# Summing the value rows' squares in the token stage, and the gate's logits right behind the taps

## The chip, the cores and the metric

The kernel runs on one core of one Trainium2 chip. The time is that of one execution on the device in microseconds; three runs of the kernel before gave 1456.38 to 1456.81 us, with a median of 1456.58 us. The engines are called by the profile's names: PE is TensorE, DVE VectorE, ACT ScalarE, POOL GpSimd, and SP is the queue that issues nearly all DMA transfers. PEld is PE's loading of weights.

## The reference

Two branches read the same tokens x (2048 x 576, float32) and are mixed by a gate. Cut to what matters:

```python
g = sigmoid((x * gate_w).sum(-1, keepdims=True))        # one logit per token
# branch a: a state space convolution, by FFT
P = exp(dt * A * l);  K = einsum("dn,dnl,dn->dl", C, P, dt * B).real
a = irfft(rfft(x, 2L) * rfft(K, 2L))[:L] + x * Dskip
# branch b: product key experts, 32 heads, 64 x 64 = 4096 experts
q1, q2 = split(x @ w_q);  s1 = q1 @ k1.T;  s2 = q2 @ k2.T   # per head: 64 + 64 scores
e = best 2 of the 4 sums of the 2 best of s1 and the 2 best of s2
w = softmax(score[e]) * gelu(x . u[e])
b = sum over heads and both e of w * v[e]
out = g * a + (1 - g) * b
```

The value rows v are 4096 x 576. The kernel works in pairs of float16 words (a high half and a low half), so every operand gets a scale, a power of two, from a bound on its size. For v the bound is the square root of the sum of all its squares; that sum is what the change moves, beside the gate's logits.

## The kernel before

The kernel is one body for one core. Its Python code is a planner: every stage is a generator that issues instructions and yields the time for which it wants to sleep. `mm` (line 207) issues a matmul and adds its estimated cost to a clock; `pump` (line 220) resumes every generator whose time has come. An `Engine` (line 118) adds up the estimated cost of each ACT, DVE and POOL instruction, and `ready(x)` (line 235) sleeps until the estimate says that x is there. So the order of instructions on each engine is written out when the kernel is built, from estimated costs; on the chip each engine runs its list in order and waits on semaphores where the estimate was too early. Almost all instructions go through two helper lines: L134 for ACT, DVE and POOL, L214 for matmuls. A DMA goes through L205; SP takes them in order, so that a transfer that waits holds up those behind it.

The stages, by the tiles that show them in the profile:

- Main loop (line 1719). PE takes turns between scores (`s`, 128 groups of query weights by tokens), act matmuls (`a`, the products of all tokens with all expert rows u, 128 triples) and whatever the other stages ask for. DVE finds the two best of each score row (MAX8, FIND_INDEX8); ACT or DVE scale the act results into `go`, which goes to DRAM as `g_d`. The last 26 act triples are held back till the scores are done.
- Token stage, `u_stage1` (line 1063). The first half of the FFT of the tokens, 16 rounds. A round loads two row blocks into `us`, splits them into half words `uh` (ACT writes the high, DVE the low halves), does 12 matmuls `u`, copies the results and stores them as `su_d`. Its pace is tied to the K stage. When it is through, its memory `uf` is closed.
- K stage (`k_front`, `k_gen`, `k_store`). The convolution's kernel, in 36 chunks, on all engines: PE (`kP`, `kb`), ACT (exponentials and sines), POOL and DVE. Each pair of chunks ends in a bank `kb` and a store `k_d`. When all are stored and the token stage has closed its memory, `freq` starts.
- `freq` (line 1265). It loads the stored chunks ("the taps", `ksb`, four DMAs), starts `v_norm` 40 us and `gating` 20 us later, runs `k_stage1` (the FFT of the taps, tiles `k` and `k1o`, stored as `sk_d`), and then `products` (line 1164): 36 rounds of matmuls `pr` and `pi`, multiplications on POOL or DVE (`tt`, `vf`), matmuls `pv`, copies `vo` and stores `z_d`.
- `v_norm` (line 1396). 32 blocks of value rows are loaded (tile `vn`), squared and summed by ACT (`ju`, shown as `vj`). After them one matmul `pvn` sums over partitions and gives v's scale. Then 16 blocks of tokens are loaded into the same tile, four DMAs each, multiplied by the gate's weights on POOL and summed by ACT; the sigmoid over `gA` ends it.
- `gating` (line 981), eight rounds, one per chunk of heads: the two experts of each head and their softmax (tiles `gg...`), on POOL, DVE and ACT. The last round also turns the results for the next stage (`tr`, `placed`).
- `v_work` (line 1444), started behind `k_stage1`: eight chunks of value rows are loaded and split into half words `vhl`, ACT writing the high and DVE or POOL the low halves. It needs v's scale (`vnormed`), and memory: three chunks' places are opened with it, two more behind `products`, the last three when both `gated` and `gates` are set. A chunk is loaded into the place of the one after it; the eighth into a slot, as `vs`.
- Output stage (line 1767), from the first `o` matmul on. For each of 16 token tiles `prep` builds one-hot factors on DVE (`A`, `Be`, `Bg`), PE multiplies them (`S`, 64 columns each), DVE multiplies by the activations `gl`, ACT and DVE split the result into `wh`, and 192 matmuls `o` multiply `wh` with all of `vhl`. `y_part` adds the inverse FFT (`yz`, `y`, `ya`).

What decides when the last places for value rows open (lines 1298 to 1305):

```python
        spawn(prep(0))
        v_pool(3, 5)
        while not gated or not gates:
            yield 0.5
        FG.__exit__(None, None, None)
        WJ.__exit__(None, None, None)
        v_pool(5, 8)
        shut.append(1)
```

and what `v_work` waits for (lines 1453 to 1460):

```python
            while not vnormed or c not in vt or (c < 7 and c + 1 not in vt):
                yield 1
            if c not in raw:
                if c == 7:
                    yield from need("slot")
                load(c)
            if c + 2 in vt or (c == 6 and done(need("slot"))):
                load(c + 1)
```

Of the kernel before, what the change touches and what calls it, by code (L numbers as in the profile page):

```python
# [24 lines left out]
D = 576  # L25
# [113 lines left out]
def body(ctx: ExitStack, tc: tile.TileContext, xT, au, par, logdt, dskip, gatew, wq, kT, uT, vv,  # L139
# [60 lines left out]
    def dma(o, i, q=None):  # L200
        t = max(clock[0], rdy.get(key(i), 0.0), queue[0])
        queue[0] = t + 0.45
        wire[0] = max(wire[0], t) + (2 if o.dtype in (F16, BF16) else 4) * o.shape[0] * size(o) / 3.4e5
        rdy[key(o)] = max(rdy.get(key(o), 0.0), wire[0] + 2.2)
        (q or DQ).dma_start(o, i)  # L205
# [10 lines left out]
    def spawn(gen, after=0.0):  # L216
        heapq.heappush(heap, (clock[0] + after, nseq[0], gen))
        nseq[0] += 1
# [94 lines left out]
    def au_load(a, t):  # L313
        for d, o in au_rows(au, t, a):
            dma(o, d)
# [747 lines left out]
    def u_stage1():  # L1063
        nonlocal uf
        yield from need("slot")
        us = slot([4, D], F32, "us")
        columns.add(us.tensor.name)
        s_u, i_u = root_scale(nx2, 1.02)
        ended = [0]
        ld = {}  # L1070

        def load(p):
            a = us[:, p % 2, :]
            for g in range(2):
                l, far = U_PAIRS[2 * p + g]
                dma(a[64 * g:64 * g + 64], bass.AP(tensor=au.tensor, offset=au.offset + l * D,
                                                   ap=[[64 * D, R1], [(far - l) * D, 2], [1, D]]))
            tu = uf.tile([128, 2, 128], F16, tag="tu", name=f"tu{p}", bufs=2)
            dma(tu, tu_d[:, p])
            ld[p] = a, tu  # L1080

        def tail(p, tag, pbs):
            for g in range(2):
                o = us[:, 2 + g, :]
                for hh in range(2):
                    pb = pbs[hh][g]
                    yield from ready(pb)
                    ov = o[:, 288 * hh:288 * hh + 288]
                    S.activation(ov, pb[:, :288], AF.Copy)
                    free(tag, ov)  # L1090
                yield from ready(ov)
                dma(pair_rows(su_d, 2 * p + g), o)
            ended[0] += 1

        load(0)
        for p in range(NT):
            a, tu = ld.pop(p)
            yield from ready(a, tu)
            while ended[0] < p - 1:
                yield 0.3  # L1100
            h = uf.tile([128, 2, D], F16, tag="uh", name=f"uh{p}", bufs=2)
            S.activation(h[:, 0], a, AF.Copy, scale=s_u)
            yield from ready(h)
            V.scalar_tensor_tensor(h[:, 1], a, s_u, h[:, 0], op0=OP.mult, op1=OP.subtract)
            if p + 1 < NT:
                load(p + 1)
            yield from ready(h)
            while ended[0] < p:
                yield 0.3
            tag = side()  # L1110
# [12 lines left out]
            yield 12  # L1123
        while ended[0] < NT:
            yield 1
        free("slot")
        quota(raw=2)
        while not kstored[0]:
            yield 1
        V.scalar_tensor_tensor(iuk, iuk, 2.0 ** -28, i_u, op0=OP.mult, op1=OP.mult)  # L1130
        UF.__exit__(None, None, None)
        uf = 0
# [132 lines left out]
    def freq():  # L1265
        nonlocal ff, ab, iota_a, iota_b
        ff = FG.__enter__()
        wrems.append(ff.tile([128, 2, 512], F16, name="wrem3"))
        V.memset(wrems[3][64:128, 1, :], 0.0)
        ksb = KS.__enter__().tile([128, 4, NCK // 2, 32, 2 * NI], F16, name="ksb")  # L1270
        fk = FK.__enter__()
        tabs = [fk.tile([128, 16, 2, 128], F16, tag="tk", name=f"tk{w0}", bufs=2) for w0 in (0, 16)]
        for w0, tkt in zip((0, 16), tabs):
            dma(tkt, tk_d[:, w0:w0 + 16, :])
        for j in range(4):
            while wire[0] > clock[0] + 2:
                yield 0.3
            dma(ksb[:, j].rearrange("p c w i -> p c (w i)"),
                k_d[:, 32 * j:32 * j + 32].rearrange("c l z m n -> (l z m) c n"))
        spawn(v_norm(), 40)  # L1280
        spawn(gating(0), 20)
        yield from k_stage1(ksb, fk, tabs)
        FK.__exit__(None, None, None)
        KS.__exit__(None, None, None)
        v_pool(0, 3)
        spawn(v_work())
        fp = FP.__enter__()
        quota(sc=3, wb=5)
# [105 lines left out]
    vt = {}  # L1394

    def v_norm():
        ld = {}

        def load(b):
            a = ff.tile([128, D], F32, tag="vn", name=f"vn{b}", bufs=2)  # L1400
            if b < 32:
                dma(a, vv[128 * b:128 * b + 128])
            else:
                au_load(a, b - 32)
            ld[b] = a

        gw = row(gatew, "gw", ff)
        load(0)
        for b in range(48):
            if b + 1 < 48:  # L1410
                load(b + 1)
            a = ld.pop(b)
            yield from ready(a)
            ju = ff.tile([128, D], BF16, tag="ju", name=f"vj{b}")
            if b < 32:
                S.activation(ju, a, AF.Square, accum_out=vsum[:, b:b + 1])
            else:
                G.tensor_mul(a, a, gw)
                yield from ready(a)
                S.activation(ju, a, AF.Copy, accum_out=gA[:, b - 32:b - 31])  # L1420
            yield 2
            if b != 31:
                continue
            V.tensor_reduce(out=nut[:, 2:3], in_=vsum, axis=AX, op=OP.add)
            yield from ready(nut)
            tag = side()
            yield from need(tag)
            p = bank(tag, "pvn")
            mm(p[:, 0:1], onesb, nut.bitcast(BF16)[:, 5:6], True, True, 0.05)
            yield from ready(p)  # L1430
            sv.extend(root_scale(p[:, 0:1], 1.02))
            free(tag, sv[0])
            vnormed.append(1)
            del p
        S.activation(gA, gA, AF.Sigmoid)
        gates.append(1)

# [402 lines left out]
```

## Time and profile before

| | |
|---|---|
| median of three runs | 1456.58 us |
| the profiled execution's own time | 1458.63 us |
| its span, first to last instruction | 1456.8 us |
| mean granted PE clock | 0.998 of full speed |
| PE busy | 1430.8 us, 98% |
| DVE busy | 1221.0 us, 84% |
| ACT busy | 776.0 us, 53% |
| POOL busy | 521.4 us, 36% |
| HBM | 141.74 MB read, 71.30 MB written |

All positions are in microseconds from the span's start. A group of instructions is named by what it writes and reads, without buffer numbers: `vj<-vn` is the squaring of value rows. Behind a bar a group shows its total busy time, the mean length of one instruction in ns, and the idle time of its engine just before. A view of waits gives the waiting engine and tile, what it waited for, the total, the number of waits and the longest. In a view of time a bracket behind an instruction is the idle time before it, and what ended it. A view of stretches gives, for each, the busy time of every engine with the number of instructions, then the granted clock of PE, the mean busy share of the DMA engines, and GB/s. A view of one tile gives least, median and longest duration in ns, and the starts of the first and the last instruction.

Busy PE does not mean that PE works at its peak: small matmuls, and matmuls at a low clock, count as busy.

### The profile page before, as it was taken

How to read it: one execution, taken by the hardware profiler on the slowest of the kernel's cores; microseconds unless marked ns; L12 is line 12 of the kernel's file. 1: busy time of each engine (PE TensorE's matmuls, PEld its weight loads, DVE VectorE, ACT ScalarE, POOL GpSimd, SP SyncE). 2: the span in 40 equal slices, each digit the busy share in tenths (PEclk: the TensorE clock that was granted, in tenths of full speed). 3: DMA queues.
4: the chain of work that ended last, by engine and by line, in shares of the span. 5: the costliest groups of instructions: out<-in, count | busy, mean ns of one | idle time of the engine just before them, and what ended most of it. 6: DMA issues, size and time to landing. Idle time of an engine off the chain costs nothing.

```text
span 1456.8 us, 36814 instructions
## 1 busy us (share of the span) xinstructions
PE 1430.8 (98%) x14103; PEld 853.9 (59%) x14105; DVE 1221.0 (84%) x4569; ACT 776.0 (53%) x1304; POOL 521.4 (36%) x510
## 2 busy tenths in 40 slices
PE   7999999999999999999999999999899999999998
PEld 3445445555454445455555444447687887888787
DVE  6898889889877996885989898689998988998860
ACT  6346776796685776834556564576333224323310
POOL 0335357536446446210237999623000100110100
PEclk9999999999999999999999999999999999999999
DMA  8235223442434432269486776787343432342400
GB/s 306 77 112 172 88 80 109 126 138 72 129 106 124 116 104 92 62 211 292 157 304 216 266 250 214 255 265 228 130 122 110 140 120 98 125 148 67 157 9 17
DMA packets 134352, 215.44 MB, mean 148 GB/s; under 512 B 10912, under 2 KB 79904, under 8 KB 127776
## 3 DMA queue, kind: packets, MB, share of 16 engines
q1 hardware_dynamic: 134080, 213.01, 45.3%
q8 instruction: 111, 1.82, 0.5%
q14 instruction: 65, 0.53, 0.1%
q10 hardware_dynamic: 96, 0.07, 0.0%
HBM read 141.74 MB, written 71.30 MB: 146 GB/s over the span
## 4 chain that ended last, share of the span: by engine, by line
PE 85%; DVE 5%; DMA 2%; ACT 1%; issue 0%; POOL 0%; SPq 0%; DVEq 0%; POOLq 0%
PE o L214 25%; PE s L214 22%; PE a L214 22%; PE S L214 4%; PE kb L214 2%; PE wb L214 2%; PE pr L214 2%; DMA vn<-in_au_dram 1%; PE y L214 1%; PE kP L214 1%; PE k L214 1%; DVE i L134 1%; PE pv L214 1%; PE u L214 1%; DVE vhl L134 1%; DVE m L134 1%
## 5 line engine op out<-in xcount | busy, mean ns | idle before, releaser
L214 PE MATMUL o<-vhl,wh 128*128 128x288 f16 x3072 | 389.2, 287 | 0.0
L214 PE MATMUL s<-whl,xb 128*128 128x512 f16 x1536 | 365.0, 379 | 0.0
L214 PE MATMUL a<-xb,uhl 128*128 128x512 f16 x1536 | 359.5, 379 | 0.2 <-DVE go L134 0.2
L214 PEld LDWEIGHTS <-wh 128*128 128x128 f16 x3072 | 296.8, 98 | 77.5 <-issue 3.7
L214 PEld LDWEIGHTS <-xb 128*128 128x128 f16 x1792 | 170.6, 98 | 208.5 <-issue 14.3
L214 PEld LDWEIGHTS <-uhl 128*128 128x128 f16 x1536 | 147.1, 98 | 176.3 <-issue 3.2
L134 DVE FIND_INDEX8 i<-m,s 128x8 uint32<-128x64 f32 x1024 | 206.9, 226 | 0.0
L134 ACT ACTIVATE wh<-gl,s_wg 128x1024 f16<-128x1024 f32 x64 | 69.0, 1137 | 203.6 <-DVE gl L134 203.6
L134 DVE MAX8 m<-s 128x8 f32<-128x64 f32 x1024 | 146.4, 217 | 27.1 <-PE s L214 26.6
L134 POOL TENSOR_TENSOR CS<-CS,ex 128x512 f32<-128x512 f32 x72 | 97.9, 1389 | 147.6 <-DVE ex L134 146.2
L134 POOL TENSOR_TENSOR ya<-ya,db 128x576 f32<-128x576 f32 x16 | 31.8, 1995 | 320.3 <-DVE Bg L134 159.2
L134 ACT ACTIVATE go<-a,i_a 128x512 f32<-128x512 f32 x92 | 61.5, 682 | 89.1 <-PE a L214 63.9
L134 DVE TENSOR_TENSOR gl<-S,gl 128x256 f32<-128x256 f32 x256 | 90.3, 416 | 13.5 <-PE S L214 10.1
L134 POOL TENSOR_TENSOR e<-aN,rt 128x512 f32<-128x512 f32 x72 | 83.1, 1174 | 49.9 <-PE kb L214 43.8
L134 DVE SCALAR_TENSOR_TENSOR wh<-gl,s_wg,wh 128x1024 f16<-128x1024 f32 x64 | 91.1, 1455 | 11.3 <-ACT wh L134 11.3
L134 DVE TENSOR_TENSOR Bg<-Be,vals 128x1024 f16<-128x1024 f16 x128 | 91.7, 758 | 2.2
L134 ACT ACTIVATE gl<-gl 128x1024 f32<-128x1024 f32 x64 | 63.4, 1044 | 34.1 <-DMA gl<-g_d 34.1
L214 PE MATMUL S<-Bg,A 128*128 128x64 f16 x2048 | 73.6, 194 | 6.4 <-DVE Bg L134 6.4
L214 PEld LDWEIGHTS <-A 128*128 128x128 f16 x2048 | 71.4, 98 | 11.4 <-DVE Bg L134 4.9
L134 DVE TENSOR_TENSOR A<-iota_a,vals 128x2048 f16<-128x2048 f16 x64 | 77.9, 1218 | 0.0
L134 DVE MATCH_VALUE_LOAD i<-m,s 128x8 f32 x1024 | 76.3, 75 | 0.1
L214 PE MATMUL s<-wrem,xb 128*128 128x512 f16 x256 | 76.2, 379 | 0.0
(206 smaller groups left out, 2156.6 us busy)
## 6 DMA issues: line engine op xcount, KB each, us to landing
g_d<-go SPq DMA_DIRECT2D x128, 256.0 KB, 2.4
gl<-g_d SPq DMA_DIRECT2D x32, 1024.0 KB, 5.5
wq<-in_wq_dram SPq DMA_DIRECT2D x16, 1152.0 KB, 5.6
su_d<-us SPq DMA_DIRECT2D x32, 288.0 KB, 2.6
sk_d<-k1o SPq DMA_DIRECT2D x32, 288.0 KB, 3.7
vn<-in_vv_dram SPq DMA_DIRECT2D x32, 288.0 KB, 4.1
ui<-su_d SPq DMA_DIRECT2D x16, 576.0 KB, 4.0
ki<-sk_d SPq DMA_DIRECT2D x16, 576.0 KB, 5.5
```

The lines of the kernel that those rows point to most:

```text
L134: return f(*a, **k)
L214: T.matmul(o, l, r, start=start, stop=stop)
```

## The change

The former `v_norm` is cut in two.

- The squares of the value rows, with the matmul and the scale behind them, are now `v_norm` alone. It is started in the token stage, right behind the first load. It has one place for its block, in the token stage's memory; ACT writes the squares over the block. Each of the 32 rounds loads, waits for the load, squares, and pauses for 9 us. The token stage closes its memory only when it is done.
- The gate is now `gate`, started 4 us behind the issue of the last tap load, with two places for the block as before, and the same DMAs, multiplications and sums.
- The half words `uh` of the token stage have one place where they had two, which gives the place for the block (2304 bytes a partition in both cases).

```diff
         load(0)
+        spawn(v_norm())
         for p in range(NT):
...
-            h = uf.tile([128, 2, D], F16, tag="uh", name=f"uh{p}", bufs=2)
+            h = uf.tile([128, 2, D], F16, tag="uh", name=f"uh{p}", bufs=1)
...
-        while ended[0] < NT:
+        while ended[0] < NT or not vnormed:
             yield 1
...
-        spawn(v_norm(), 40)
+        spawn(gate(), 4)
         spawn(gating(0), 20)
...
     def v_norm():
+        for b in range(32):
+            a = uf.tile([128, D], F32, tag="vn", name=f"vn{b}", bufs=1)
+            dma(a, vv[128 * b:128 * b + 128])
+            yield from ready(a)
+            S.activation(a, a, AF.Square, accum_out=vsum[:, b:b + 1])
+            yield 9
+        V.tensor_reduce(out=nut[:, 2:3], in_=vsum, axis=AX, op=OP.add)
...
+        vnormed.append(1)
+
+    def gate():
         ld = {}
 
-        def load(b):
-            a = ff.tile([128, D], F32, tag="vn", name=f"vn{b}", bufs=2)
-            if b < 32:
-                dma(a, vv[128 * b:128 * b + 128])
-            else:
-                au_load(a, b - 32)
-            ld[b] = a
+        def load(t):
+            ld[t] = ff.tile([128, D], F32, tag="vn", name=f"xg{t}", bufs=2)
+            au_load(ld[t], t)
 
         gw = row(gatew, "gw", ff)
         load(0)
-        for b in range(48):
...
+        for t in range(NT):
+            if t + 1 < NT:
+                load(t + 1)
+            a = ld.pop(t)
             yield from ready(a)
...
+            ju = ff.tile([128, D], BF16, tag="ju", name=f"gj{t}")
+            G.tensor_mul(a, a, gw)
+            yield from ready(a)
+            S.activation(ju, a, AF.Copy, accum_out=gA[:, t:t + 1])
             yield 2
...
         S.activation(gA, gA, AF.Sigmoid)
         gates.append(1)
```

More of the change, by code (lines that the diff above doesn't have):

```diff
@@ new lines, in v_norm @@
+        V.tensor_reduce(out=nut[:, 2:3], in_=vsum, axis=AX, op=OP.add)
+        yield from ready(nut)
+        tag = side()
+        yield from need(tag)
+        p = bank(tag, "pvn")
+        mm(p[:, 0:1], onesb, nut.bitcast(BF16)[:, 5:6], True, True, 0.05)
+        yield from ready(p)
+        sv.extend(root_scale(p[:, 0:1], 1.02))
+        free(tag, sv[0])
+        vnormed.append(1)
+    def gate():
+        ld = {}
+        def load(t):
+            ld[t] = ff.tile([128, D], F32, tag="vn", name=f"xg{t}", bufs=2)
+            au_load(ld[t], t)
@@ L1407, in v_norm @@
         gw = row(gatew, "gw", ff)
         load(0)
-        for b in range(48):
-            if b + 1 < 48:
-                load(b + 1)
-            a = ld.pop(b)
+        for t in range(NT):
+            if t + 1 < NT:
+                load(t + 1)
+            a = ld.pop(t)
             yield from ready(a)
[L1414 to L1420, printed above, removed]
-            yield 2
[L1422 to L1434, printed above, removed]
+            ju = ff.tile([128, D], BF16, tag="ju", name=f"gj{t}")
+            G.tensor_mul(a, a, gw)
+            yield from ready(a)
+            S.activation(ju, a, AF.Copy, accum_out=gA[:, t:t + 1])
+            yield 2
```

## The prediction

> **What bounds the kernel now.** I read the page's busy table first, then the waits of TensorE (PE: us, times, longest), then PE in order of time around its longest wait, and last DVE and the change's own instructions.
>
> ```profile
> PE 1430.8 (98%) x14103; PEld 853.9 (59%) x14105; DVE 1221.0 (84%) x4569; ACT 776.0 (53%) x1304; POOL 521.4 (36%) x510
> ```
>
> PE is the bound: 26.0 us of the 1456.8 us span are all that it is not busy, and the change leaves every matmul in place. So the change can pay only in PE's waits, and in stretches where its clock is low. The waits of PE, by what ended them:
>
> ```profile
> PE sq L214 <- ACT xb L134: 9.1, 3, 5.0
> PE S L214 <- DVE Bg L134: 6.4, 4, 4.6
> ...
> PE kb L214 <- issue: 1.6, 1, 1.6
> PE pi L214 <- DVE i L134: 1.3, 1, 1.3
> ```
>
> The 9.1 us are the opening, ahead of everything that the diff touches. The largest other item is S waiting for DVE's Bg, 4.6 us of it in one place. PE in order of time there, and the stretches with the granted clock (columns: PE, PEld, DVE, ACT, POOL busy, clock, DMA share, GB/s; a 1.65 us wait lies in the first of the three):
>
> ```profile
> 963.98 1.10 PE L214 MATMUL S<-Bg,A 128*128 128x64 f16 x31 [1.02 <-DVE Bg L134]
> ...
> 1019.53 3.84 PE L214 MATMUL o<-vhl,wh 128*128 128x288 f16 x30
> 1027.94 0.23 PE L214 MATMUL S<-Bg,A 128*128 128x64 f16 x1 [4.57 <-DVE Bg L134]
> 1028.53 1.81 PE L214 MATMUL S<-Bg,A 128*128 128x64 f16 x31 [0.36 <-DVE Bg L134]
> 1030.16 5.95 PE L214 MATMUL o<-vhl,wh 128*128 128x288 f16 x30
> ```
> ```profile
> 450.00:460.00 10.00, 8.36 (x175) 4.93 (x170) 5.50 (x10) 5.68 (x11) 10.00 (x10) 1.00 0.58 181
> 1020.00:1030.00 10.00, 5.06 (x58) 4.04 (x56) 9.97 (x17) 1.38 (x2) 2.62 (x2) 0.88 0.94 329
> 1030.00:1040.00 10.00, 10.00 (x95) 7.41 (x93) 8.36 (x17) 2.19 (x3) 0.00 (x0) 0.78 0.14 35
> ```
>
> PE waits 4.57 + 0.36 = 4.9 us, and then pays again: 30 o matmuls take 5.95 us where 30 took 3.84, and 31 S matmuls 1.81 against 1.10, together 2.8 us at a granted clock of 0.88 and 0.78. This place costs 7.7 us, and DVE (the third busy column) is busy 9.97 of 10 us in it. DVE's groups from 940 to 1030, and then three of the same groups from 1100 to 1400, where POOL does almost nothing:
>
> ```profile
> L134 DVE TENSOR_TENSOR Bg<-Be,vals 128x1024 f16<-128x1024 f16 x22 | 20.7, 982 | 0.4
> L134 DVE SCALAR_TENSOR_TENSOR wh<-gl,s_wg,wh 128x1024 f16<-128x1024 f32 x8 | 13.2, 1674 | 0.0
> L134 DVE TENSOR_TENSOR Be<-iota_b,vals 128x1024 f16<-128x1024 f16 x11 | 9.8, 892 | 0.0
> L134 DVE SCALAR_TENSOR_TENSOR vhl<-vhl,sci,vhl 128x576 f16<-128x576 f32 x11 | 9.1, 845 | 0.8 <-issue 0.8
> L134 DVE SCALAR_TENSOR_TENSOR vhl<-vs,sci,vhl 128x576 f16<-128x576 f32 x3 | 4.7, 1577 | 0.0
> ```
> ```profile
> L134 DVE TENSOR_TENSOR Bg<-Be,vals 128x1024 f16<-128x1024 f16 x84 | 55.6, 703 | 1.5
> L134 DVE SCALAR_TENSOR_TENSOR wh<-gl,s_wg,wh 128x1024 f16<-128x1024 f32 x42 | 59.4, 1444 | 9.4 <-ACT wh L134 9.4
> L134 DVE TENSOR_TENSOR Be<-iota_b,vals 128x1024 f16<-128x1024 f16 x42 | 28.8, 686 | 0.0
> ```
>
> Two things make DVE late. It still splits value rows (vhl): 9.1 + 4.7 = 13.8 us. And its instructions are long here: 22 x 0.28 + 11 x 0.21 + 8 x 0.23 = 10.3 us over their later means.
>
> **Why the value rows are split so late.** The last five chunks need v_pool(5, 8), which opens only when the gate is done. What the tile vn leaves, the last gating step, the end of the products, and the gate's sigmoid with a table load on each side of it:
>
> ```profile
> L205 SPq DMA_DIRECT2D vn<-in_au_dram x64: 310/419/2223, 825.6 to 955.7; - x64
> L134 ACT ACTIVATE vj<-vn x48: 666/683/732, 715.1 to 961.7; 128x576 bf16<-128x576 f32 x48
> L134 ACT ACTIVATION_READ_ACCUMULATOR vj<-vn x48: 185/192/243, 715.6 to 962.3; 128x1 f32 x48
> L205 SPq DMA_DIRECT2D vn<-in_vv_dram x32: 327/349/622, 709.6 to 820.2; - x32
> L134 POOL TENSOR_TENSOR vn<-vn,gw x16: 1395/1412/1846, 838.7 to 959.4; 128x576 f32<-128x576 f32 x16
> 929.57 0.32 POOL L134 TENSOR_TENSOR vals<-ggu,ggd 128x64 f32<-128x64 f32 x1
> 931.48 0.35 SPq L205 DMA_DIRECT2D z_d<-vo  x1
> 962.52 1.28 ACT L134 ACT_TABLE_LOAD   x1
> 963.82 0.22 ACT L134 ACTIVATE gA<-gA 128x16 f32<-128x16 f32 x1
> 992.71 0.51 SPq L205 DMA_DIRECT2D vs<-in_vv_dram  x1
> ```
>
> Gating is through at 929.6 and the products at 931.5; the gate comes at 962, so it alone holds the pool back by some 30 us, and the last chunk (vs) is loaded at 992.7 and split on DVE just ahead of the late Bg.
>
> **The change part by part.**
>
> *Gate behind the taps.* It starts 4 us after the last tap load is issued, near 675 by my estimate (the last k_d store stands at 641.7 below, four loads follow it), and not behind 32 value blocks. An iteration is a load ahead, 1.41 us of POOL, 0.68 + 0.19 us of ACT and a pause of 2 us: I estimate 5 us, 16 of them 80 us, so an end near 755 to 760, well before 930. The pool then opens near 932. From its opening (962.5) to the load of vs took 30 us; kept at that pace the load comes near 962, or when a slot comes free, at the latest with the last act matmul, ahead of the first o matmul. Either way vhl's end leaves the last microseconds ahead of the late Bg. The 1.28 us table loads around the sigmoid move too. Of the 16 POOL multiplies, spread evenly from 838.7 to 959.4, about four fall past 930 into DVE's crowded stretch, and leave it.
>
> Its cover: products are POOL's stage, and gate multiplies leave it.
>
> ```profile
> 650.00:700.00 50.00, 50.00 (x438) 27.40 (x437) 32.03 (x188) 22.00 (x48) 2.73 (x9) 1.00 0.86 281
> 700.00:750.00 50.00, 50.00 (x334) 27.48 (x333) 45.14 (x346) 31.20 (x96) 11.57 (x39) 1.00 0.68 222
> 850.00:900.00 50.00, 48.29 (x456) 22.85 (x449) 46.49 (x280) 25.83 (x71) 48.67 (x44) 1.00 0.58 192
> 80.00:480.00 400.00, 395.34 (x3740) 196.19 (x3739) 349.79 (x1460) 279.74 (x418) 207.60 (x168) 1.00 0.36 111
> ```
>
> POOL is busy 48.67 of 50 us from 850 on and 2.73 of 50 from 650 on. SP's queue takes 64 x 0.42 = 27 us of gate issues into 674 to 760, among the tap results' stores; a load there waits for ACT two rows back, and stores behind it wait along. On POOL, gating's short steps now stand behind a multiply of 1.41 us at times. PE has scores to do meanwhile, 50.00 of 50 us busy: nothing on the path. The products may start some us late (value chunks now load beside their first inputs, as v_work no longer polls for the norm) and run some 15 us less on POOL (about ten multiplies of 1.41 us ahead of 915). I take these as cancelling.
>
> *Squares in the token stage.* 32 blocks, each one DMA of 0.35 us on SP (11 us in all), 0.68 + 0.19 us of ACT (28 us), and a pause of 9 us. With some 3 us for a load an iteration is 12 us, the whole 390 us, from the stage's start some 10 us ahead of its first uh to about 475; its last uh is written at 626.4, so the new condition `not vnormed` holds nothing. ACT is busy 280 of 400 us there, and would be 308. There is one place for the block, so SP's load waits for the square before; that was issued 9 us earlier by the plan, and k_d, g_d and wq transfers queue behind it if ACT is later than that. ACT in turn waits for loads with its other work behind. The nearest row is the same loop with two places, from 715 on:
>
> ```profile
> ACT vj L134 <- DMA vn<-in_vv_dram: 8.9, 8, 2.1
> ```
>
> that is 0.28 us a block. What reaches PE lies between 0 (one kb wait of 1.6 us is all that PE shows of the K chain now, with 120 us of ACT idle) and the 12 of 18 kb banks that fall ahead of 475 (evenly from 183.3 to 641.7), each late by a square and its wait, 12 x (0.87 + 0.28) = 13.8 us. A gain is excluded, since nothing leaves this stage. I take 2.0, near the row with the one wait.
>
> *One place for the half words.* The 16 writes (and the 18 stores of K banks, used above and below), then the u matmuls that read one place and ACT's next write:
>
> ```profile
> L134 ACT ACTIVATE uh<-us,sci x16: 759/764/785, 92.1 to 626.4; 128x576 f16<-128x576 f32 x16
> L205 SPq DMA_DIRECT2D k_d<-ko x18: 332/333/477, 183.3 to 641.7; - x18
> ...
> 117.35 0.79 PE L214 MATMUL u<-uh,tu 64*128 64x288 f16 x10 [1.41 <-DVE uh L134]
> 128.69 0.78 ACT L134 ACTIVATE uh<-us,sci 128x576 f16<-128x576 f32 x1
> ```
>
> The write comes 10 us after the last read (118.1 to 128.7): nothing, unless that distance is used up.
>
> *The sum*, against the profiled execution's 1458.63 us: gap 4.9, its slow clock 2.8, the S wait at 964 in the same crowd 1.0, half of the 1.3 us wait of the products' pi on DVE 0.65; against it 2.0 in the token stage and 1.5 for a wait that stays in the o stage (the four S waits less the long one are 1.8). 1458.63 - 9.35 + 3.5 = 1452.8. The median of the runs, 1456.58, is 2.05 us below the profiled execution: **1450.7 us**.
>
> [...] A 1.65 us wait left the clock at 1.00, the 4.57 us one brought 0.78. [...] No run here shows a gap between the two.
>
> **Rivals.** *The gap stays.* PE runs its list in order, and the S group stands where the plan thought DVE done; the plan moves up with the free pool and DVE is again behind it. For it: DVE has no free time around 1020. Against: 13.8 us of splitting leave the stretch or move up. Then only the 0.65 and the 2.0 are left: 1456.6 - 0.65 + 2.0 = 1457.9, the same within 0.2% (2.9 us, about what a measurement of this kernel tells from no change).
>
> *Slower: ACT holds up the K chain.* The 13.8 us bound comes true in the token stage, while the rest goes as forecast: 1456.6 - 9.35 + 1.5 + 13.8 = 1462.5. It decides from the point where PE waits some 11 us more between 80 and 480 than its 4.7 now. For it: ACT runs in order and every block's load is issued just in time. Against: ACT is free 30% there, and PE has four banks of other work.
>
> [...]
>
> **How the numbers follow.** Forecast 0.54, gap stays 0.12, K chain 0.24, contention moves 0.10; so faster 0.54, same 0.12, slower 0.34. Range: down to all gains, the products' waits whole and no cost, 1456.6 - 4.9 - 2.8 - 1.0 - 1.3 = 1446.6, and 1.6 more if the kb wait goes too, 1445.0; up to 1463, which takes in the gap that stays, the moved contention and the K chain's price. The forecast's own range is 1445 to 1454.
>
> **What would show it.** Right: gA's sigmoid near 760, pvn near 475, vs loaded before 992, no PE wait over 2 us from 1000 to 1050 and clock 1.00 there, POOL below 45 of 50 us from 850 to 900. Wrong: PE's waits from 80 to 480 above 11 us, the last k_d store well behind 641.7, or a long S wait again with a low clock behind it.

## The result, and the profile after

The change makes the kernel slower. Five runs of the changed kernel took 1470.89 to 1474.82 us, with a median of 1471.59 us; five runs of the kernel before, on the same chip, have a median of 1456.38 us. The ratio is 1.0109, with a 95% interval from 1.0094 to 1.0124; 0.0109 of 1456 is 16 us. The forecast was 1450.7 us, and its range ended at 1463.0.

The profiled execution of the changed kernel took 1470.89 us, its span is 1469.0 us, and its mean granted clock 0.994. Its busy table, for TensorE's line:

```profile
PE 1436.6 (98%) x14103; PEld 855.3 (58%) x14105; DVE 1224.4 (83%) x4590; ACT 769.5 (52%) x1285; POOL 514.6 (35%) x510
```

The number of matmuls is the same. PE's idle time went from 26.0 to 1469.0 - 1436.6 = 32.4 us, and its busy time rose by 5.8 us for the same matmuls. So the loss has two halves: new waits, and matmuls that take longer. The waits of PE (us, times, longest) in the changed kernel:

```profile
PE sq L214 <- ACT xb L134: 9.2, 3, 5.1
PE S L214 <- DVE Bg L134: 4.6, 5, 2.0
PE a L214 <- DVE wrem L134: 3.1, 1, 3.1
PE wn L214 <- ACT k1o L134: 2.5, 1, 2.5
PE kb L214 <- issue: 2.4, 1, 2.4
```

The long wait for Bg is gone, as forecast: no S wait is over 2.0 us. But three single waits are new or longer. PE in order of time at these places, and at the S waits that stay:

```profile
309.81 0.39 PE L214 MATMUL a<-xb,wrem 128*128 128x512 f16 x1 [3.10 <-DVE wrem L134]
...
490.13 0.26 PE L214 MATMUL kb<-Y,CS 128*32 128x64 f32 x4 [2.41 <-issue]
...
693.84 0.19 PE L214 MATMUL wn<-sc,onesb 128*128 128x1 bf16 x2 [2.51 <-ACT k1o L134]
...
1009.77 0.20 PE L214 MATMUL S<-Bg,A 128*128 128x64 f16 x1 [2.01 <-DVE Bg L134]
...
1040.62 0.20 PE L214 MATMUL S<-Bg,A 128*128 128x64 f16 x1 [1.36 <-DVE Bg L134]
1041.21 1.59 PE L214 MATMUL S<-Bg,A 128*128 128x64 f16 x31 [0.40 <-DVE Bg L134]
```

The clock (third column from the end) falls behind all of them but the one at 490:

```profile
310.00:320.00 10.00, 10.00 (x161) 5.17 (x160) 5.43 (x6) 9.94 (x16) 6.58 (x6) 0.83 0.18 42
490.00:500.00 10.00, 9.87 (x62) 4.74 (x63) 5.40 (x24) 9.94 (x13) 2.23 (x3) 1.00 0.19 55
690.00:700.00 10.00, 7.25 (x27) 3.05 (x25) 4.66 (x32) 4.58 (x12) 3.65 (x6) 0.67 0.86 297
1010.00:1020.00 10.00, 9.63 (x89) 7.55 (x89) 9.93 (x20) 6.28 (x7) 1.58 (x2) 0.83 0.39 116
1040.00:1050.00 10.00, 8.99 (x108) 7.21 (x109) 9.58 (x21) 0.70 (x1) 0.00 (x0) 0.83 0.69 246
```

The same execution by long stretches (columns: length, then PE, PEld, DVE, ACT, POOL busy, clock, DMA share, GB/s), first of the kernel before, then of the changed one:

```profile
50.00:640.00 590.00, 585.29 (x5500) 289.49 (x5500) 517.31 (x2309) 401.92 (x602) 283.29 (x229) 1.00 0.35 107
640.00:760.00 120.00, 120.00 (x888) 64.31 (x886) 96.61 (x676) 61.62 (x162) 16.22 (x55) 1.00 0.78 263
760.00:960.00 200.00, 198.06 (x1968) 97.63 (x1965) 167.64 (x863) 117.48 (x312) 165.01 (x189) 1.00 0.70 235
960.00:1100.00 140.00, 133.63 (x1437) 96.28 (x1436) 135.21 (x202) 69.81 (x85) 24.12 (x15) 0.98 0.58 184
```
```profile
50.00:640.00 590.00, 580.03 (x5460) 286.84 (x5460) 510.13 (x2169) 418.82 (x655) 280.06 (x229) 1.00 0.41 125
640.00:760.00 120.00, 116.41 (x840) 61.53 (x839) 99.75 (x733) 56.80 (x155) 32.79 (x57) 0.97 0.70 226
760.00:960.00 200.00, 198.83 (x1937) 97.09 (x1936) 169.16 (x955) 96.86 (x248) 147.94 (x189) 1.00 0.57 199
960.00:1100.00 140.00, 135.43 (x1437) 94.80 (x1436) 129.19 (x197) 63.88 (x77) 23.36 (x14) 0.98 0.57 184
```

PE is idle 5.3 us more in the first stretch and 3.6 us more in the second, and 0.8 and 1.8 us less in the others. The time lost at a low clock, estimated as PE's busy time times what the clock lacks of 1.00 over stretches of 10 us, is 2.8 us before (all from 1020 to 1040) and 7.4 us after: 1.7 at 310, 2.5 at 690, 3.2 between 1010 and 1050. Idle +6.4 (32.4 less 26.0) and clock +4.6 make 11.0 of the 12.2 us by which the span is longer. So the loss lies in the token stage and around the taps, in front of the place at which the prediction looked.

The same is seen from the first `o` matmul, at 995.3 before and at 1011.7 after. The row up to it and the row from it, before and after:

```profile
0.00:995.30 995.30, 978.32 (x8950) 489.85 (x8953) 847.75 (x3977) 637.88 (x1162) 485.33 (x491) 1.00 0.51 165
995.30:1456.80 461.50, 452.47 (x5159) 364.06 (x5155) 373.21 (x593) 138.11 (x144) 36.06 (x19) 0.99 0.35 112
```
```profile
0.00:1011.70 1011.70, 985.09 (x8984) 492.22 (x8987) 857.11 (x4008) 637.40 (x1151) 484.36 (x493) 0.99 0.51 163
1011.70:1469.00 457.30, 451.49 (x5124) 363.03 (x5121) 367.30 (x584) 132.06 (x135) 30.28 (x17) 0.99 0.35 111
```

The output stage gains 4.2 us (by an estimate about 1 us of it because some 34 more matmuls lie ahead of it; 32 of S take 1.13), and all ahead of it loses 16.4.

What the prediction said would show the steps, in the changed kernel's views of the single tiles (least, median, longest in ns, first and last start):

```profile
L134 ACT ACTIVATE vn<-vn x32: 665/674/708, 93.0 to 513.8; 128x576 f32<-128x576 f32 x32
L214 PE MATMUL pvn<-nut,onesb x1: 166/166/166, 524.8 to 524.8; 128*128 128x1 bf16 x1
L134 POOL TENSOR_TENSOR xg<-xg,gw x16: 1397/1404/1428, 690.9 to 778.8; 128x576 f32<-128x576 f32 x16
L134 ACT ACTIVATE gA<-gA x1: 215/215/215, 787.9 to 787.9; 128x16 f32<-128x16 f32 x1
L205 SPq DMA_DIRECT2D vs<-in_vv_dram x1: 373/373/373, 991.9 to 991.9; - x1
```

The gate is done 176 us sooner. Gating ends at 938.2 (before 929.6) and the products' last store is issued at 939.0 (before 931.5), so the last places for value rows open 23 us sooner (939 against 962.5); yet the last chunk is loaded at 991.9, as before.

### The profile page after: what moved, and what is told of

Its sections match the earlier page's. It is cut to its first block, busy times and chain, and to the rows that moved or that the text cites. A ratio compares the mean times of both kernels' runs of the same rounds, so it can differ in the third digit from the quotient of the medians.

```text
span 1469.0 us, 36780 instructions
## 1 busy us (share of the span) xinstructions
PE 1436.6 (98%) x14103; PEld 855.3 (58%) x14105; DVE 1224.4 (83%) x4590; ACT 769.5 (52%) x1285; POOL 514.6 (35%) x510
## 4 chain that ended last, share of the span: by engine, by line
PE 83%; DVE 7%; DMA 2%; issue 1%; ACT 0%; SPq 0%; DVEq 0%; ACTq 0%
PE o L214 24%; PE a L214 23%; PE s L214 21%; PE S L214 4%; PE kb L214 2%; PE pr L214 2%; PE wb L214 2%; DVE i L134 2%; PE kP L214 1%; PE pv L214 1%; DVE m L134 1%; PE y L214 1%; PE k L214 1%; PE u L214 1%; DMA wq<-in_wq_dram 1%
## 5 line engine op out<-in xcount | busy, mean ns | idle before, releaser
L214 PEld LDWEIGHTS <-xb 128*128 128x128 f16 x1792 | 171.1, 98 | 209.5 <-issue 16.1
L134 DVE SCALAR_TENSOR_TENSOR wh<-gl,s_wg,wh 128x1024 f16<-128x1024 f32 x64 | 87.8, 1404 | 11.3 <-ACT wh L134 11.3
L134 ACT ACTIVATE go<-a,i_a 128x512 f32<-128x512 f32 x81 | 55.0, 685 | 78.9 <-PE a L214 53.1
L214 PE MATMUL a<-xb,wrem 128*128 128x512 f16 x256 | 76.3, 380 | 3.7 <-DVE wrem L134 3.1
```

Source lines behind the costliest of these rows:

```text
L134: return f(*a, **k)
L214: T.matmul(o, l, r, start=start, stop=stop)
```

## The experiments

Two theories were set against each other. **The moved work**: squares on ACT and loads on SP in the token stage, and the gate's DMAs around the taps, hold up PE by their own length. **The lists**: every engine runs a list whose order the planner wrote from estimated costs; a moved start changes the clock at which each generator wakes, so the order of nearly everything behind it changes, and the kernel before has a list in which the waits happen to fall well. Ratios are to the kernel before in the same comparison; its medians there were 1456.38 to 1458.74 us.

**Each part alone.** The gate behind the taps, with the squares where they were, in two places of their own (shown in part, against the kernel before):

```diff
         spawn(v_norm(), 40)          # the 32 squares alone
+        spawn(gate(), 4)
...
```

> Only the gate is moved behind the taps; the squares stay where they were, started 40 us behind the taps, with two places of their own, and uh has its two places. Theory Q (the gate's 64 loads on SP hold up the tap results' stores, and PE behind them): PE again waits 2 us or more with a clock below 0.8 between 680 and 700, about 6 us lost there, partly given back in the output stage (4 us): 1456 to 1462 us. Theory T (the squares in the token stage are the loss): no loss here, and the output stage's gain stays, 1450 to 1454 us.

Measured: 1475.03 us, ratio 1.0115 (1.0097 to 1.0132), above what either theory gave. PE is busy 113.19 of 120 us from 640 to 760, and the token stage is as before (586.44 of 590).

The squares in the token stage, and the gate where its old start would put it:

```diff
-        spawn(gate(), 4)
+        spawn(gate(), 155)
```

> Squares in the token stage as in the change, but the gate starts 155 us behind the last tap load instead of 4, which is about where it ran before. Theory T: the token stage still loses some 7 us to PE waits between 260 and 320 and near 490, the taps' stage loses nothing: 1463 to 1466 us. Theory Q: 1456 to 1460 us, as the gate's loads are out of the taps' way.

Measured: 1466.89 us, 1.0058 (1.0041 to 1.0075). From 50 to 640 PE is busy 580.32 us, as little as in the change, with the same waits for wrem (3.1) and kb (2.5). So each part loses, each in its own stretch: the squares about 5 us of idle and 3.1 us of low clock there, the gate mostly from 640 to 760.

The half words' one place, alone:

```diff
-            h = uf.tile([128, 2, D], F16, tag="uh", name=f"uh{p}", bufs=2)
+            h = uf.tile([128, 2, D], F16, tag="uh", name=f"uh{p}", bufs=1)
```

> The kernel before with one place for uh instead of two; the instructions of every engine stand in the same order. All theories: no change, 1455 to 1458 us, since ACT writes a round's halves some 10 us behind the last matmul that reads the round before.

Measured: 1456.75 us, 0.9988 (0.9977 to 0.9999). The order on all engines is the same as before, and so is the time: this step of the prediction holds.

**The squares taken away.** With the change, loads and squares are replaced by a constant and a pause as long as the whole loop:

```diff
-        for b in range(32):
-            a = uf.tile([128, D], F32, tag="vn", name=f"vn{b}", bufs=1)
-            dma(a, vv[128 * b:128 * b + 128])
-            yield from ready(a)
-            S.activation(a, a, AF.Square, accum_out=vsum[:, b:b + 1])
-            yield 9
+        V.memset(vsum, 1.44)
+        yield 390
```

> The change with the 32 loads and squares of the value rows left out (a constant stands for their sums, so this part is not computed); the gate stays behind the taps, uh has one place. Theory T: the 306 us wait and its slow clock go, 7 us less than the change: 1463 to 1466 us. Theory Q: 1469 to 1472 us, as the change.

Measured: 1468.04 us, 1.0073 (1.0053 to 1.0094). It has less to do than the kernel before, and is 9.3 us slower than its runs beside it. The work of the squares can't be the reason, and at the gate's place, from 640 to 760, PE is idle for 1.2 us only. Its loss lies elsewhere: 7.0 us of waits for Bg, and 3.7 us of low clock from 960 to 1100. The wait for wrem is gone, as theory T had it, but other waits have come.

The squares without their loads (one block squared 32 times, the gate at 155 us):

```diff
+        V.memset(vsum, 1.44)
+        a = uf.tile([128, D], F32, tag="vn", name="vn0", bufs=1)
+        dma(a, vv[0:128])
+        yield from ready(a)
         for b in range(32):
-            a = uf.tile([128, D], F32, tag="vn", name=f"vn{b}", bufs=1)
-            dma(a, vv[128 * b:128 * b + 128])
-            yield from ready(a)
-            S.activation(a, a, AF.Square, accum_out=vsum[:, b:b + 1])
-            yield 9
+            S.activation(a, a, AF.Square, accum_out=col32[:, b:b + 1])
+            yield 12
```

> As the run with the squares alone in the token stage (gate at 155 us), but one block is loaded once and squared 32 times, 12 us apart; 31 of the 32 loads are left out, and a constant stands for the sums. Theory T-work (ACT's 28 us of squares make the K chain and the half words late): still a wait of 2 us or more on wrem or kb between 260 and 500, 1463 to 1468 us. Theory T-load (ACT waits for the loads, 13.6 us in the change, and passes that on): those waits go, 1457 to 1461 us.

Measured: 1483.5 us, 1.0170 (1.0141 to 1.0199). The token stage has no more idle time than before, although ACT squares as much as in the change:

```profile
50.00:640.00 590.00, 586.75 (x5496) 290.15 (x5495) 524.14 (x2332) 417.52 (x654) 281.35 (x229) 1.00 0.34 107
...
960.00:1100.00 140.00, 121.42 (x1316) 84.83 (x1315) 123.71 (x184) 76.43 (x105) 40.23 (x23) 0.95 0.57 184
```

All of its loss is past 760, most of it from 960 on: here the gate ends at 983.3 and the last chunk is loaded at 1014.9. The two forecasts were 1463 to 1468 and 1457 to 1461 us, and the loss lies where neither put it.

**The gate's loads on another queue.**

```diff
-            au_load(ld[t], t)
+            for d, o in au_rows(au, t, ld[t]):
+                dma(o, d, nc.scalar)
```

> The change, with the gate's 64 token loads issued from ACT's queue instead of SP's. Theory Q (SP's order holds the tap results back behind the gate's loads): the 2.5 us wait near 690 and the low clock behind it go, some 6 us: 1464 to 1467 us. Rival A (ACT itself is late there, because the gate's sums and the loads' issue lie on it): the waits of PE on k1o stay or grow: 1470 us or more.

Measured: 1477.02 us, 1.0121 (1.0094 to 1.0148). The wait of wn goes, but k now waits 2.4 us for the tap loads and 2.0 us for ACT, and PE is busy 114.69 of 120 us from 640 to 760, where the change has 116.41. The compute instructions of every engine stand in the change's order here, by the names in the traces; only the queues of SP and ACT differ. So moving the loads off SP's queue doesn't win back what is lost there.

**A later gate.**

```diff
-        spawn(gate(), 4)
+        spawn(gate(), 40)
```

> The change with the gate started 40 us behind the taps instead of 4, so past the first tap results and still ahead of the products. Theory Q: no wait near 690, the token stage's loss of some 7 us stays and the output stage's gain too, 1463 to 1467 us. Rival L: anything from 1457 to 1480 us, with waits in other places than in the change from the taps on.

Measured: 1471.01 us, 1.0082 (1.0061 to 1.0102). PE's busy time from 640 to 760 rises to 119.00 us, and falls from 760 to 960 to 195.14. The loss moves with the gate.

**Starts moved in the kernel before, no work moved.** These runs ask what a change of the lists costs by itself.

```diff
-        spawn(v_norm(), 40)
+        spawn(v_norm(), 44)
```

> The kernel before with the value rows' squares started 44 us behind the taps instead of 40; nothing else. It moves no work between stages. Theories Q and T, which put the loss down to where the work lies: within 3 us of before, 1454 to 1460 us. Rival L (the list written out by the plan is re-dealt by any change of a start, and the kernel before is a good deal among many): 1460 us or more, with other waits than before.

Measured: 1486.46 us, 1.0183 (1.0157 to 1.0209), the costliest edit of the kernel before. Its largest wait and the stretch around the first `o` matmuls:

```profile
PE S L214 <- DVE Bg L134: 17.6, 7, 6.1
```
```profile
1000.00:1050.00 50.00, 32.28 (x356) 23.96 (x357) 47.99 (x70) 21.67 (x28) 17.12 (x10) 0.71 0.69 227
```

The gate ends at 985.3 here, 21.5 us later than before, and the last chunk is loaded at 1035.1, 42 us later. So a late gate, a late last chunk and long waits for Bg stand together, as the prediction's mechanism has it. But the run doesn't price that mechanism alone: all five engines have another order, and from 1019.0 to 1035.0 SP issues other loads of the output stage ahead of the last chunk.

The token stage started 1 us later:

```diff
-        spawn(u_stage1(), 1)
+        spawn(u_stage1(), 2)
```

> The kernel before with the token stage started 2 us behind the fourth token block instead of 1; nothing else. Theories Q and T: within 3 us of before, 1454 to 1460 us. Rival L: 1460 us or more, with other waits than before.

Measured: 1456.87 us, 0.9991 (0.9970 to 1.0013). By the names in the traces no list changes, and the time stays. This is below the 1460 us that rival L named: not every moved start deals the lists anew.

`v_norm` 3 us sooner:

```diff
-        spawn(v_norm(), 40)
+        spawn(v_norm(), 37)
```

> The kernel before with the squares started 37 us behind the taps instead of 40; nothing else. Rival L: a few us or more slower than before, as with 44; waits of S on Bg above before's. If it stays within 3 us of before, the loss with 44 was that of a late gate, and not of any new deal.

Measured: 1481.65 us, 1.0167 (1.0144 to 1.0189). All engines have another order; the losses lie from 760 to 960 (190.24 of 200 us busy) and in 11.2 us of waits for Bg.

`v_norm` 2 us later. By the names in the traces this leaves the lists of PE, DVE and POOL as they are; one instruction of ACT and one transfer of SP stand elsewhere:

```diff
-        spawn(v_norm(), 40)
+        spawn(v_norm(), 42)
```

> The kernel before with v_norm started 42 us behind the tap loads in place of 40. The lists of DVE and POOL stay, those of PE and ACT change in a few places. The order theory expects the time of before, 1455 to 1460. If what cost 28.8 us with 44 is the later start of the norm and the gate themselves, half of it should come: about 1470.

Measured: 1459.24 us, 1.0006 (0.9992 to 1.0021). With 2 us nothing happens, with 4 us nearly 29 us are lost. What costs is the new order, not the later start.

**Other lists of the changed kernel.** The pause between two squares, 9 us in the change:

```diff
-            yield 9
+            yield 8                  # and 10, and 11
```

> The change with a pause of 8 us between the squares instead of 9; the same work in the same stages, in another order. Rival L: the token stage's 5 us of waits (306 and 490) are gone or elsewhere, and the time lies anywhere from 1455 to 1480 us. Theories T and Q (the work's place counts): 1469 to 1474 us.

> The change with a pause of 10 us. As for 8: by rival L anywhere from 1455 to 1480 us with other waits, by T and Q 1469 to 1474 us.

> The change with a pause of 11 us. As for 8: by rival L anywhere from 1455 to 1480 us with other waits, by T and Q 1469 to 1474 us.

Measured: 1487.09 us, 1.0194 (1.0172 to 1.0215) with 8; 1480.52 us, 1.0152 (1.0133 to 1.0171) with 10; 1475.66 us, 1.0120 (1.0098 to 1.0142) with 11. The time doesn't follow the pace of the squares, and the waits are others each time (with 8: 16.1 us for Bg and 9.7 us for wn's input; with 10: 7.1 us for kb). Two of the three lie above even the 1480 us that rival L allowed. The change's own list is the best of these four.

**The change's list kept, the moved work cut.** In these kernels the plan still counts the whole instructions, so the order on every engine stays that of the change (by the names in the traces all lists agree), but the instructions take 64 of 576 columns:

```diff
-            S.activation(a, a, AF.Square, accum_out=vsum[:, b:b + 1])
+            planned(S, a, 0.085 + 0.00083 * D + 0.15, a)     # the plan's cost of the whole
+            nc.scalar.activation(a[:, :64], a[:, :64], AF.Square, accum_out=vsum[:, b:b + 1])
```

> The change with every engine's instructions in the same order, but each square of value rows reads 64 of its 576 columns (the other columns' squares are not computed; the plan still counts the whole). Theory T-work (the squares' length on ACT is what makes wrem and kb late): the 3 us wait near 306 and its slow clock go, 1466 to 1468 us. Rival L (it is the re-dealt order of the list): the wait stays, 1470 to 1473 us.

Measured: 1468.49 us, 1.0067 (1.0044 to 1.0091), between the two forecasts. The two waits of the token stage stay, with squares a ninth as wide:

```profile
309.17 0.39 PE L214 MATMUL a<-xb,wrem 128*128 128x512 f16 x1 [3.51 <-DVE wrem L134]
...
489.76 0.26 PE L214 MATMUL kb<-Y,CS 128*32 128x64 f32 x4 [2.68 <-issue]
```

The same with the loads cut too, each to 64 columns:

> As the run with the short squares, and each load brings 64 of 576 columns too (the rest of the value rows' sums is left out). Theory T-load: waits on wrem and kb go that the short squares alone leave, 1464 to 1468 us. Rival L: 1470 to 1473 us, as the order is unchanged.

Measured: 1471.45 us, 1.0078 (1.0054 to 1.0102), and both waits again (3.5 and 2.5). ACT's own wait for the blocks falls from 13.6 us in the change to 5.5 us, and PE gains nothing by it.

The gate's loads, multiplications and sums cut in the same way, the squares whole:

> The change with every engine's instructions in the same order, but the gate's loads, multiplications and sums work on 64 of 576 columns (the rest of the gate's logits is left out). Theory Q (the gate's transfers hold SP and the tap results): the waits near 690 and the low clock go, some 6 us: 1464 to 1467 us. Rival L: they stay, 1470 to 1473 us.

Measured: 1467.48 us, 1.0061 (1.0040 to 1.0081). The wait of wn falls from 2.5 to 0.6 us and the clock stays at 1.00 from 680 to 710; the waits for wrem and kb stay (3.1 and 3.0), and of PE's idle time from 640 to 760 2.0 of 3.6 us stay.

All of it cut, the squares, their loads and the gate:

> The kernel with the change, every instruction where it was, but all that the change moved cut to a ninth: the 32 loads and squares of value rows, and the gate's loads, multiplications and sums, take 64 of 576 columns (the other columns are left out, so scale and gate come from a ninth of the sums; the plan still counts them whole). If the 16 us come from the order of the lists, a good part stays: 1463 to 1470. If they come from the work in its new places, nearly all goes: 1456 to 1460.

Measured: 1468.38 us, 1.0076 (1.0053 to 1.0099). The stretches of this run:

```profile
50.00:640.00 590.00, 578.27 (x5327) 284.84 (x5326) 508.17 (x2143) 405.98 (x653) 279.81 (x229) 0.99 0.37 111
640.00:760.00 120.00, 117.83 (x979) 63.58 (x977) 103.82 (x770) 52.47 (x158) 17.19 (x58) 1.00 0.58 193
```

The idle time stays (11.7 and 2.2 us in these two stretches, where the kernel before has 4.7 and none); of the low clock 2.5 of 7.4 us stay. So with the order kept and the work cut to a ninth, 0.76% of the 1.09% remain: about 11 of 16 us lie in the order, and about 5 in the length of the moved work, with intervals that just overlap. This split is rough: the squares alone cut left 1.0067, the gate alone cut 1.0061, no more than with all of it cut, so the 5 us can't be shared out among the parts. What the runs don't separate is what the 32 short squares, the short gate and the DMA issues still cost in these kernels; the kernel without squares has none of the squares' part and loses as much (1.0073), but in another list.

Over all the runs: each edit that left the lists of before (nearly) alone gave 0.9988 to 1.0006, and each that changed them gave 1.0058 to 1.0194, with more work, less work or the same. No kernel tried is faster than the one before by more than 0.12%.

## Why the prediction was wrong

**The step that failed first** is one that stands in no term: the sum took the profile of before and altered it only in the places that the change touches ("the change leaves every matmul in place"). Each matmul is there, but not in its place. The plan of the changed kernel has another order on all engines, and the runs price this at about 11 us here, and at 23 and 29 us for starts moved by 3 and 4 us. The place that the prediction chose to mend, 7.7 us, is worth less than the new list cost here.

**"PE has scores to do meanwhile: nothing on the path"** (the gate behind the taps) failed. PE was busy 50.00 of 50 us there before, but it runs its list in order: in the changed kernel the scores that start at 695.24 stand behind wn, which waits 2.51 us, and they cover none of it. From 640 to 760 it lost 3.6 us of idle time and 2.5 us of clock. The prediction had named the queue: gate loads stand on SP among the tap results' stores.

```profile
680.58 9.39 SPq L205 DMA_DIRECT2D xg<-in_au_dram  x8
690.07 0.40 SPq L205 DMA_DIRECT2D g_d<-go  x1
690.56 5.42 SPq L205 DMA_DIRECT2D sk_d<-k1o  x7
```

Seven stores of k1o wait behind eight gate loads of 9.39 us; the copies into k1o wait for stores (2.16 us on ACT at 693.4, 5.96 us on DVE), and PE's wn waits 2.51 us for ACT's copy. With the gate cut to a ninth the wait is 0.6 us and the clock 1.00 from 680 to 710, so this part is the gate's own; with its loads on ACT's queue other waits took its place. The chance of 0.10 for "contention moves", and its share in the range up to 1463, took the moved multiplications on POOL to hold up DVE; no run shows that term. From 690 to 785, beside the moved multiplications, DVE's nine copies into k1o took 457 ns in the mean, and four took 454 ns before.

**The token stage at 2.0** failed by size: 5.3 us of idle and 1.7 us of clock, 7.0 us. It lies inside the bound of 13.8, but not by the mechanism of that bound. The rival "ACT holds up the K chain" would have shown PE's waits from 80 to 480 above 11 us and the last k_d store behind 641.7; they were 7.5 us there and the store came at 640.8, and the waits don't shorten with the squares. In the trace, ACT has the exponentials and sines of two K pairs back to back from 297 to 316 with one wrem between them, at 305.6; the last square ahead of it ended at 294.7. DVE writes the other half of wrem at 309.0, behind two groups of Y and e. That is an order of the list; it was seen, and not tried by itself.

**"Kept at that pace"** failed. The pool opened near 939, 23 us sooner, near the forecast of 932. But from there to the load of vs took 53 us where it took 30 before, and the load stood at 991.9 and not near 962. So freeing the memory sooner didn't bring the last chunk sooner. The loads of the third to the seventh chunk, ahead of vs, before and after:

```profile
934.78 1.04 SPq L205 DMA_DIRECT2D vhl<-in_vv_dram  x2
...
962.53 0.92 SPq L205 DMA_DIRECT2D vhl<-in_vv_dram  x2
...
980.11 0.54 SPq L205 DMA_DIRECT2D vhl<-in_vv_dram  x1
```
```profile
943.07 0.94 SPq L205 DMA_DIRECT2D vhl<-in_vv_dram  x2
...
957.08 0.43 SPq L205 DMA_DIRECT2D vhl<-in_vv_dram  x1
...
962.87 0.84 SPq L205 DMA_DIRECT2D vhl<-in_vv_dram  x1
...
977.92 0.50 SPq L205 DMA_DIRECT2D vhl<-in_vv_dram  x1
```

Before, two of these chunks were loaded 28 us ahead of the opening, so the 30 us behind it were those of the last four chunks. After, all six come behind it: the places of the first two open with the end of the products, and that came 7.5 us later. From the first of the six to vs took 58 us before and 49 after. So the gate was not the only thing that held the last chunk back; the end of the products and the way from chunk to chunk behind it stood next, and what sets the pace of that way isn't settled. DVE still had as much of these splits to do next to the late Bg:

```profile
L134 DVE SCALAR_TENSOR_TENSOR vhl<-vhl,sci,vhl 128x576 f16<-128x576 f32 x12 | 11.2, 960 | 0.0
...
L134 DVE SCALAR_TENSOR_TENSOR vhl<-vs,sci,vhl 128x576 f16<-128x576 f32 x2 | 1.6, 806 | 0.0
```

11.2 + 1.6 = 12.8 us of splits from 940 to 1030, where it was 13.8.

**The gap and its clock** were right in kind and too large: the 4.57 us wait is gone, S waits fell from 6.4 to 4.6 us, and the stage from the first `o` matmul gained 4.2 us, where the sum had 4.9 + 2.8 less 1.5. The low clock stayed there: 3.2 us of it where 2.8 had been, behind shorter waits.

**The clock behind a shorter gap.** The prediction had the clock at 1.00 behind 1.65 us of waiting and at 0.78 behind 4.57 us, nothing between the two, and its sum counted the whole 2.8 us of slow clock as saved. Here gaps of 2.0 us and less brought 0.83 over 10 us; the halved gap saved its wait and not its clock.

**Right**: one place for the half words costs nothing; POOL was busy 44.60 of 50 us from 850 to 900, below the 45 named; the products lost nothing by themselves (760 to 960 gained 0.8 us). **Too early by the estimates**: the gate took 5.9 us a block and not 5, since POOL waited 73 us for its loads, and began 6 us later, with its first load at 680.6, so its sigmoid came at 787.9 and not at 760; a square's round took 13.6 us and not 12 ((513.8 - 93.0) / 31), so pvn came at 524.8 and not at 475; a load landed 3.2 us (median) after its issue, near the 3 taken, and at most 8.0. No wait of PE shows that either came too late.

## What to carry to other kernels

Where a planner writes each engine's order from estimated costs, a new start is a new program: before pricing a gain of a few microseconds, ask whether the order elsewhere stays, and measure what moving a start with no work costs; here that is within the measurement when the order stays and 23 to 29 us when it doesn't. A busy engine that runs in order covers no wait with work that stands behind it in its list: PE, 50.00 of 50 us busy before, lost 2.51 us to one late copy with scores behind it. And to tell moved work from moved order, keep the plan's costs and shrink the work: what stays is the order.

## What the runs showed of the hardware

The clock fell behind shorter gaps than the 4.57 us of before, and later than the gap: a wait of 2.01 us ended at 1009.77 and one of 0.40 us at 1010.37, and the clock fell at 1010.82. PE in the changed kernel, microsecond by microsecond, from the 2.01 us wait on (a wait of 0.40 us lies in the second row):

```profile
1009.00:1010.00 1.00, 0.20 (x1) 0.11 (x2) 0.98 (x2) 0.00 (x0) 0.00 (x0) 1.00 0.00 0
1010.00:1011.00 1.00, 0.63 (x19) 0.63 (x19) 1.00 (x3) 0.00 (x0) 0.00 (x0) 0.91 0.02 8
1011.00:1012.00 1.00, 1.00 (x19) 0.91 (x17) 1.00 (x5) 0.92 (x2) 0.00 (x0) 0.50 0.00 0
...
1014.00:1015.00 1.00, 1.00 (x9) 0.74 (x7) 1.00 (x4) 0.46 (x1) 0.00 (x0) 0.88 0.29 84
1015.00:1016.00 1.00, 1.00 (x11) 0.80 (x9) 1.00 (x2) 1.00 (x2) 0.00 (x0) 1.00 0.07 28
```

The first matmuls behind the wait still have the full clock; from about 1010.8 on it is 0.50, and from 1014.2 on 1.00 again (0.09 / 0.5 + 3 + 0.12 / 0.5 = 3.4 us). So these 2.0 us of waiting cost, by an estimate from the 3.41 us at 0.50, about 1.7 us more, hidden in busy time. It doesn't follow from the length of the wait alone: 1.36 + 0.40 us at 1040 cost the same (0.50 from 1041.54 to 1044.95), a wait of 2.41 us at 490 left the clock at 1.00 in the changed kernel, and behind one of 2.68 us at the same place, with the short squares, it was 0.83 over 10 us.

When it falls can be read from the trace. In the changed kernel the clock falls at 311.09, 693.38, 1010.82 and 1041.54, and once more behind the last matmul, at 1468.21. The first four times lie 112, 93 and 9 times 3.413 us apart, and the clock stays at 0.50 for 3.41, 6.83, 3.41 and 3.41 us. The stretch of one such step ahead of each fall, and the slow one behind it, with the three steps around the 2.41 us wait at 490 between them:

```profile
307.67:311.09 3.42, 1.28 (x6) 0.60 (x7) 2.83 (x6) 3.40 (x5) 1.91 (x2) 1.00 0.43 178
311.09:314.50 3.41, 3.41 (x9) 1.22 (x8) 0.00 (x0) 3.40 (x4) 3.41 (x3) 0.50 0.00 0
485.16:488.58 3.42, 2.56 (x120) 1.85 (x116) 0.75 (x1) 3.35 (x7) 1.45 (x2) 1.00 1.01 330
488.58:492.00 3.42, 1.87 (x22) 0.97 (x23) 0.22 (x1) 3.40 (x5) 3.06 (x4) 1.00 0.06 16
492.00:495.41 3.41, 3.41 (x20) 1.72 (x19) 2.87 (x6) 3.40 (x4) 0.59 (x1) 1.00 0.27 79
689.96:693.38 3.42, 1.37 (x8) 0.58 (x6) 0.00 (x0) 1.26 (x2) 2.46 (x2) 1.00 0.77 260
693.38:700.21 6.83, 6.13 (x20) 2.64 (x20) 4.66 (x32) 3.57 (x10) 1.41 (x5) 0.50 0.89 309
1007.40:1010.82 3.42, 1.01 (x18) 0.56 (x17) 3.38 (x4) 0.00 (x0) 1.04 (x1) 1.00 0.01 2
1010.82:1014.23 3.41, 3.41 (x33) 2.51 (x30) 3.38 (x12) 1.35 (x2) 0.00 (x0) 0.50 0.26 76
1038.12:1041.54 3.42, 1.67 (x22) 1.12 (x20) 3.39 (x5) 0.00 (x0) 1.17 (x1) 1.00 0.90 248
1041.54:1044.95 3.41, 3.41 (x36) 2.57 (x33) 3.38 (x7) 0.00 (x0) 0.00 (x0) 0.50 1.01 417
```

In the steps ahead of the four falls PE was idle for 2.14, 2.05, 2.41 and 1.75 us. The wait at 490 lies in two steps of the same grid, which is 52 steps behind 311.09 at 488.58: 0.86 us of idle time in one and 1.55 in the other, and the clock stayed at 1.00. In the kernel before, with a grid laid through its one fall at 1027.64 in the same steps, the 1.65 us wait lies in one step (454.20 to 457.62) and cost nothing, and the step ahead of the fall was idle throughout. In these two traces, from 60 us to 8 us before the end, 809 steps are at the full clock: the 5 with 1.75 us of idle PE or more were followed by a slow one each time, the 804 with 1.65 us or less never. So in these two traces a step's idle time tells the falls apart, and the length of a wait alone doesn't (2.01 + 0.40 us was paid twice, 2.41 us was not). Five falls are few, and no run moved one wait against the grid.
